# A planner's lists for the first layer, drawn up anew, with some order-only waits taken out

## The chip, the cores and the metric

The kernel runs on one core of a Trainium2 chip. The core has five engines with a queue of instructions each: TensorE (PE in the profile, its weight loads PEld), VectorE (DVE), ScalarE (ACT), GpSimd (POOL) and SyncE (SP), which here only issues DMAs. They are kept in step by semaphores. The metric is the device time of one execution in microseconds (us), from the launch to the last store.

## The reference

The input is x, 2048 rows of 512 values. Two kinds of blocks, A and B, are applied in turn, A B A B, each on a layernorm of its input, and each is added to its input.

```python
def _A_ref(x, wqkv, wo):            # H = 32 heads of Dh = 16
    q, k, v = ...                   # (x @ wqkv), split by head
    phi = lambda t: jnp.where(t > 0, t + 1, jnp.exp(t)) + 1e-6
    pq, pk = phi(q), phi(k)
    kv = jnp.einsum("bhsd,bhse->bhde", pk, v)
    z = jnp.einsum("bhsd->bhd", pk)
    num = jnp.einsum("bhqd,bhde->bhqe", pq, kv)
    den = jnp.einsum("bhqd,bhd->bhq", pq, z)[..., None] + 1e-6
    return (num / den) ... @ wo     # heads joined again

def _B_ref(x, w1, w2):              # 512 -> 1376 -> 512
    return jnp.maximum(x @ w1, 0) @ w2

x = x + _A_ref(_layernorm(x), wqkv, wo)
x = x + _B_ref(_layernorm(x), w1, w2)
x = x + _A_ref(_layernorm(x), wqkv, wo)
x = x + _B_ref(_layernorm(x), w1, w2)
```

A is a linear attention: no softmax over the rows, but a 16x16 matrix kv for each head, summed over all rows, which every row's phi(q) is then multiplied with.

## The kernel before, in words

**Tiles.** The 2048 rows are 16 tiles of 128 rows, and four tiles are a chunk. xin holds x in bf16, xn the normalized tiles, Tb their transposes, which the projections need as an operand. Products go to one of eight PSUM banks (ps), and ScalarE or VectorE brings them from there to SBUF.

**The first layer.** Chunk 0 (tiles 0 to 3) goes a way of its own. Its tiles are only centred (`center`, L855), transposed on TensorE (L524) and brought to Tb (`trev`, L528 and L529), and the reciprocal deviation rstd is put in later, as a scale of the evacuation. For that each tile has an own eps and an own power on GpSimd (`rstd_own`, L849 and L851). Tiles 0 to 2 have their mean and variance from bn_stats and bn_aggr on VectorE (L458, L459), tile 3 from two passes of ScalarE (L865, L867) and two small steps of GpSimd (L869, L871). Chunks 1 to 3 are normalized in full before they are transposed: bn_stats and bn_aggr of each tile on VectorE, eps on GpSimd (`veps`, L464), the power -1/2 on GpSimd (`rstd`, L466), and the normalization on VectorE (`norm`, L490). Chunk 1 does this in two pairs of tiles (4 and 5, 6 and 7) and is transposed on TensorE; chunks 2 and 3 do it four tiles at a time and are transposed by DMA.

The bn_stats of a tile in chunks 1 to 3 reads its tile of xin, and it is also told that it reads the eps result of the tile pair or chunk before (`ln_stats_first(i, [("veps1", lo - 1)])`). It doesn't use that value: this is a wait for the order alone. Tiles 4 and 5 so wait for tile 3's eps, 6 and 7 for that of 4 and 5, chunk 2 for that of 6 and 7, chunk 3 for that of chunk 2.

**phi.** Each block of k or q in a PSUM bank is brought to SBUF as phi by `phi_evac`. The usual way has two passes of ScalarE over the bank, one for t + 1 + 1e-6 (`_lin`, L551) and one for exp (`_exp`, L553), then min(exp, 1) + 1e-6 on VectorE (`_em`, L555), and the larger of both on VectorE (`_phi`, L562). Blocks that are named in the set STT leave the first pass out: VectorE takes t from the bank itself, in one scalar_tensor_tensor (L559). Before, there are two such blocks.

**After the projections** phi(k) and the rows give G (`a_g`), from it kv (`a_kv`), masked on VectorE (L650), and Mf, which is kv times wo (L657, L658). The denominators are products with a column of sums (`den`), ln and exp on ScalarE (L705, L707), spread over partitions by DMAs (`spread`, L717) and multiplied to phi(q) on VectorE (`pqs`, L723). Then come the final products with Mf (`fin`) and the residual (L580). All matmuls but warm ones and transposes are on L569.

**What sets the order.** All operations of all layers are put in a graph with their reads and writes, and with a duration for each that is a constant of the kernel. `_list_schedule` then draws up the list of each engine before anything is emitted: it goes through simulated time and takes for each engine the first operation in order of priority that can start at once, else the one that can start first. The priority is the operation's place in the program plus a number from HINTS (negative is earlier). SEQS fixes the beginning of an engine's list: each name there must come after the one before it. Durations, HINTS and SEQS so change the lists, the banks and the waits that follow from them, and no instruction's own work. Names in HINTS have the layer ahead; all those that differ are of layer 0.

SP issues the loads in the order of the program: x tile 0, x tiles 1 to 3, the key weights in two halves, chunk 1 of x, the query weights, chunks 2 and 3, the value weights, their last row (`ld_wvl`), wo.

Of the kernel before, what the change touches and what calls it, by code (L numbers as in the profile page):

```python
# [7 lines left out]
ALU = alu_op_type.AluOpType  # L8
# [4 lines left out]
PE, ACT, DVE, POOL, SP = "pe", "act", "dve", "pool", "sp"  # L13
# [31 lines left out]
WINDOW = {PE: 64, ACT: 80, DVE: 80, POOL: 12, SP: 6}  # L45


HINTS = {"0.bnag1": -115, "0.bnst15": 29, "0.bnst2": -502, "0.bnst9": -79, "0.den1": 160, "0.den2": -340, "0.g0_2_1": 107,
# [5 lines left out]

SEQS = {
    "dve": ["bnst0", "bnag0"],
    "act": ["mean_3", "trev0a", "sq_3", "trev3", "trev1", "k3_exp", "k3_lin", "k1_exp", "k1_lin", "k0_exp", "q0_3_lin",
            "k2_exp", "q0_2_lin", "k2_lin", "trev6", "q0_1_lin"],
    "pool": ["veps_0", "rstd_0", "veps_2", "nm2_3", "veps_1", "var_3", "rstd_1", "veps_3", "rstd_3", "rstd4", "veps6",
            "rstd_2"],  # L60
    "pe": ["trp0a", "warm2"],
}

STT = {"0.q2_0", "0.q3_2"}


class _Op:
# [22 lines left out]
class _Graph:  # L90
# [14 lines left out]
    def add(self, eng, emit, reads=(), writes=(), dur=100.0, lat=0.0, dma=False, name=""):  # L105
        op = _Op(eng, emit, tuple(reads), tuple(writes), dur, lat, dma, name)
        op.idx = len(self.ops)
        op.key = "%d.%s" % (self.layer, name)
        op.prio = op.idx + HINTS.get(op.key, 0)
        deps = {}  # L110
# [163 lines left out]
def build_kernel(nc, A_x, A_wqkv, A_wo, B_w1, B_w2, out, n_layers_pairs=2, A_PE_CHUNKS=0, windows=None,  # L274
# [14 lines left out]
    EPS = 1e-5  # L289
# [5 lines left out]
    with es:  # L295
        def sb(name, shape, dt):
            return es.enter_context(nc.sbuf_tensor(name, list(shape), dt))
# [33 lines left out]
        var = sb("var", [128, NT], F32)  # L331
        veps = sb("veps", [128, NT], F32)
# [3 lines left out]
        mv = sb("mv", [128, NT, 2], F32)  # L336
# [11 lines left out]
        g = _Graph()  # L348
# [17 lines left out]
        def dma(emit, reads, writes, xfer_ns, name, issue=C_SP_ISSUE, late=0.0):  # L366
            sem = es.enter_context(nc.semaphore("dsem%d" % len(dma_sems)))
            dma_sems.append(sem)

            def _emit(eng, emit=emit, sem=sem):  # L370
                return emit(eng).then_inc(sem, 16)
            op = g.add(SP, _emit, reads, writes, dur=issue, lat=xfer_ns, dma=True, name=name)
            op.seq = sem
            op.late = late
            return op
# [17 lines left out]
        def tok_view(buf, t, lo=0, hi=4):  # L393
            if t == 0 and lo == 0:
                assert hi == 1
                return buf[0][0:128].rearrange("(p n) d -> p n d", p=128)
            if t == 0:
                return buf[0][128:512].rearrange("(p n) d -> p n d", p=128)[:, lo - 1:hi - 1, :]
            return buf[0][512 * t:512 * t + 512].rearrange("(p n) d -> p n d", p=128)[:, lo:hi, :]

        def ld_x(t, lo=0, hi=4, lat=1300.0):
            dma(lambda e: e.dma_start(xin[:, 4 * t + lo:4 * t + hi, :], tok_view(A_x, t, lo, hi)),  # L402
                [], [("xin", i) for i in range(4 * t + lo, 4 * t + hi)], lat, "ld_x%d_%d" % (t, lo))
        ld_x(0, 0, 1, 100.0)
        wq_v = A_wqkv.rearrange("(c p) n -> p c n", p=128)
        ld_x(0, 1, lat=1300.0)
        for k in range(2):
            dma(lambda e, k=k: e.dma_start(wqkv[:, 2 * k:2 * k + 2, D:2 * D], wq_v[:, 2 * k:2 * k + 2, D:2 * D]),
                [], [("wk", k)], 1350.0 - 150.0 * k, "ld_wk%d" % k)
        ld_x(1, lat=1450.0)  # L410
        dma(lambda e: e.dma_start(wqkv[:, :, 0:D], wq_v[:, :, 0:D]), [], [("wq",)], 1550.0, "ld_wq")
        for t in range(2, NCH):
# [44 lines left out]
        def ln_stats_first(i, after=()):  # L457
            g.add(DVE, lambda e: e.bn_stats(bst[:, i, :], xin[:, i, :]), [("xin", i)] + list(after), [("bst", i)], C_DVE_BNST, name="bnst%d" % i)  # L458
            g.add(DVE, lambda e: e.bn_aggr(mv[:, i, :], bst[:, i, :]), [("bst", i)], [("mean", i), ("var", i)], C_DVE_SMALL, name="bnag%d" % i)  # L459

        def ln_part_first(lo, hi):
            sl = slice(lo, hi)
            tl = range(lo, hi)
            g.add(POOL, lambda e: e.tensor_scalar(veps[:, sl], mv[:, sl, 1], 0.0, EPS, ALU.max, ALU.add),  # L464
                  [("var", i) for i in tl], [("veps1", i) for i in tl], 330.0, name="veps%d" % lo)
            g.add(POOL, lambda e: e.tensor_tensor(rstd[:, sl], veps[:, sl], nhalf[:, 0:hi - lo], ALU.pow),  # L466
                  [("veps1", i) for i in tl] + [("nhalf",)], [("rstd", i) for i in tl], 480.0 + 150.0 * (hi - lo), name="rstd%d" % lo)

# [69 lines left out]
        def phi_evac(b, dst_ap, dst_key, name, tok=None):  # L538
# [5 lines left out]
            else:  # L544
                esc, ekey = xres[:, s - NSCR, 0:256].bitcast(BF16), ("xres", s - NSCR)
            stt = "%d.%s" % (g.layer, name) in STT
            sc = 1.0 if tok is None else rstd[:, tok:tok + 1]
# [55 lines left out]
        def ones_col(t):  # L603
            tl = range(4 * t, 4 * t + 4)
            g.add(POOL, lambda e: e.memset(xn[:, 4 * t:4 * t + 4, D - 1:D], 1.0),
                  [], [("xn", i) for i in tl], C_POOL_SMALL, name="onec%d" % t)
# [241 lines left out]
        def rstd_own(i, var_ap):  # L848
            g.add(POOL, lambda e: e.tensor_scalar(veps[:, i:i + 1], var_ap, 0.0, EPS, ALU.max, ALU.add),  # L849
                  [("var", i)], [("veps1", i)], 300.0, name="veps_%d" % i)  # L850
            g.add(POOL, lambda e: e.tensor_tensor(rstd[:, i:i + 1], veps[:, i:i + 1], nhalf[:, 0:1], ALU.pow),  # L851
                  [("veps1", i), ("nhalf",)], [("rstd", i)], C_POOL_POW1, name="rstd_%d" % i)

        def center(i, mu):
            g.add(DVE, lambda e: e.tensor_scalar(xn[:, i, :], xin[:, i, :], mu, None, ALU.subtract),  # L855
                  [("xin", i), ("mean", i)], [("xn", i)], C_DVE_NORM_BF, name="cent%d" % i)
            transpose_pe(i)

        def ln_first(t):
            if t == 0:  # L860
                for i in range(3):
                    ln_stats_first(i, [])
                    rstd_own(i, mv[:, i, 1:2])
                    center(i, mv[:, i, 0:1])
                g.add(ACT, lambda e: e.activation(sqscr[:, 0, :], xin[:, 3, :], ACTF.Identity, scale=INV_D, accum_out=mean[:, 3:4]),  # L865
                      [("xin", 3)], [("sqscr", 0), ("mean", 3)], C_ACT_SB_AP, name="mean_3")
                g.add(ACT, lambda e: e.activation(sqscr[:, 1, :], xin[:, 3, :], ACTF.Square, scale=INV_D ** 0.5, accum_out=s2[:, 3:4]),  # L867
                      [("xin", 3)], [("sqscr", 1), ("s2", 3)], C_ACT_SQ, name="sq_3")
                g.add(POOL, lambda e: e.tensor_tensor(nm2[:, 3:4], mean[:, 3:4], mean[:, 3:4], ALU.mult),  # L869
                      [("mean", 3)], [("nm2", 0)], 300.0, name="nm2_3")  # L870
                g.add(POOL, lambda e: e.tensor_tensor(var[:, 3:4], s2[:, 3:4], nm2[:, 3:4], ALU.subtract),  # L871
                      [("s2", 3), ("nm2", 0)], [("var", 3)], 200.0, name="var_3")
                rstd_own(3, var[:, 3:4])
                center(3, mean[:, 3:4])
                return
            step = 2 if t < FIRST_PE_CHUNKS else 4
            for lo in range(4 * t, 4 * t + 4, step):
                for i in range(lo, lo + step):
                    ln_stats_first(i, [("veps1", lo - 1)])
                ln_part_first(lo, lo + step)  # L880
            for i in range(4 * t, 4 * t + 4):
                ln_norm(i, True)
                if t < FIRST_PE_CHUNKS:
                    transpose_pe(i)
            if t >= FIRST_PE_CHUNKS:
                tr_dma(t, 2 if t == 2 else 1)
            ones_col(t)
# [3 lines left out]
        def tr_dma(t, parts=1):  # L891
            extra = list(ALL_LOADS) if tr_state["first"] else []
            tr_state["first"] = False
            transpose_chunk(t, extra, parts)
            tr_state["last"] = g.ops[-1]
# [16 lines left out]
        for t in range(3):  # L912
            ln_first(t)
# [255 lines left out]
```

## Time and profile before

| What | us |
|---|---|
| Median of three runs | 589.03 |
| Lowest and highest of them | 281.23, 1539.66 |
| Profiled execution, device time | 280.72 |
| Its span, first to last instruction | 279.0 |
| TensorE busy | 273.4 |
| ScalarE busy | 173.2 |
| VectorE busy | 141.1 |
| GpSimd busy | 50.5 |

The granted clock of TensorE was 1.00 throughout. The span is the time from the first to the last instruction; 1.7 us of the device time lie around it. Busy times are sums over the span, and engines overlap. A matmul's row is longer than its turn (0.379 us for 512 columns, though the next one starts 0.216 us later), since it counts the way through the array; so TensorE's waits are read from the starts of its matmuls.

What lands when, from the DMAs' issues and landings in the trace: tile 0 at 2.81 us, tiles 1 to 3 at 4.63, the key weights' halves at 5.32 and 6.55, chunk 1 at 7.84, the query weights at 9.29, chunk 2 at 10.57, chunk 3 at 11.92.

The first layer's A block fills about the first 57 us of TensorE's list, mixed with the beginning of what follows.

### The profile page before, as it was taken

The page shows a single profiled execution, that of the slowest core. Times are in us where ns is not written, and L with a number is a line of the kernel's source. Part 1 is how long each engine was busy: PE and PEld are TensorE (multiplying, and loading weights), DVE is VectorE, ACT ScalarE, POOL GpSimd, SP SyncE. Part 2 cuts the span into 40 slices and gives each one's busy share as a digit, 9 for nine tenths or more (in the row PEclk, how much of TensorE's full clock was granted, in tenths as well). Part 3 has the DMA queues.
Part 4 walks back from the last instruction along what each step waited for, and adds up shares of the span by engine and source line. Part 5 has one row for each costly group of instructions (what it writes and reads, how often), then busy time and mean ns, then how long its engine had stood idle before and what let it go on. Part 6 is the DMA issues. An engine that isn't in the chain of part 4 may idle for free.

```text
span 279.0 us, 4188 instructions
## 1 busy us (share of the span) xinstructions
PE 273.4 (98%) x1553; PEld 140.4 (50%) x1573; DVE 141.1 (51%) x378; ACT 173.2 (62%) x353; POOL 50.5 (18%) x132
## 2 busy tenths in 40 slices
PE   7999999999999999999999999999999999999996
PEld 3545557546544544544454455664554554454443
DVE  5899983899401362443363477279935300120222
ACT  4999996669773682677372799765884366226000
POOL 6532000035400160400040400003236100000000
DMA  7905496655810053070003030085431642021012
GB/s 225 378 19 79 89 295 197 156 124 79 152 36 0 2 94 75 1 96 0 0 8 69 0 75 0 2 187 116 78 76 22 164 80 21 0 75 22 0 75 75
DMA packets 46356, 22.62 MB, mean 81 GB/s; under 512 B 36640, under 2 KB 44800, under 8 KB 46336
## 3 DMA queue, kind: packets, MB, share of 16 engines
q1 hardware_dynamic: 46336, 22.35, 34.7%
q8 instruction: 12, 0.20, 0.3%
q14 instruction: 8, 0.07, 0.1%
HBM read 7.14 MB, written 2.10 MB: 33 GB/s over the span
## 4 chain that ended last, share of the span: by engine, by line
PE 92%; DVE 3%; DMA 1%; POOL 1%; ACT 1%; issue 1%; SPq 0%
PE ps L569 92%; DVE bst L458 2%; DMA xin<-in_A_x_dram 1%; ACT big L551 1%; POOL veps L464 0%; ACT escr L553 0%; DVE Tb L529 0%; POOL rstd L851 0%; PE ps L524 0%; DVE mv L459 0%; SPq L402 0%; DVE xn L490 0%; DVE xin L818 0%; POOL veps L849 0%; POOL var L871 0%
## 5 line engine op out<-in xcount | busy, mean ns | idle before, releaser
L569 PE MATMUL ps<-w,big 128*128 128x512 bf16 (+3 forms) x356 | 76.3, 372 | 0.4
L569 PE MATMUL ps<-Tb,w 128*128 128x512 bf16 (+1 forms) x352 | 70.8, 360 | 0.0
L798 ACT ACTIVATE big<-ps 128x512 bf16<-128x512 f32 x71 | 42.2, 596 | 24.3 <-PE ps L569 24.2
L569 PEld LDWEIGHTS ps<-w,big 128*128 128x128 bf16 (+1 forms) x363 | 35.0, 98 | 41.2 <-ACT big L798 0.3
L569 PEld LDWEIGHTS ps<-Tb,w 128*128 128x128 bf16 x352 | 34.0, 98 | 32.8
L586 ACT ACTIVATE sqscr<-xres 128x512 bf16<-128x512 f32 x48 | 29.9, 623 | 30.1 <-DVE xres L580 29.7
L580 DVE SCALAR_TENSOR_TENSOR xres<-ps,xres 128x512 f32<-128x512 f32 x32 | 21.2, 689 | 43.2 <-PE ps L569 43.2
L551 ACT ACTIVATE big<-ps 128x512 bf16<-128x512 f32 x54 | 34.3, 634 | 3.0 <-PE ps L569 3.0
L577 DVE TENSOR_TENSOR xin<-ps,xres 128x512 bf16<-128x512 f32 x15 | 10.4, 691 | 49.7 <-PE ps L569 49.7
L569 PE MATMUL ps<-wqkv,Tb 128*128 128x512 bf16 x139 | 32.8, 379 | 0.5 <-ACT Tb L528 0.3
L569 PE MATMUL ps<-big,xn 128*128 128x256 bf16 (+1 forms) x222 | 30.4, 287 | 0.1
L553 ACT ACTIVATE escr<-ps 128x512 bf16<-128x512 f32 x44 | 27.9, 635 | 1.2 <-PE ps L569 1.2
L569 PE MATMUL ps<-Tb,wqkv 128*128 128x512 bf16 x112 | 26.6, 379 | 0.0
L569 PEld LDWEIGHTS ps<-big,xn 128*128 128x128 bf16 x224 | 21.6, 98 | 9.0 <-issue 0.8
L472 POOL TENSOR_SCALAR mean<-s 128x4 f32<-128x4 f32 x12 | 3.0, 248 | 121.1 <-DVE xres L580 121.0
L569 PE MATMUL ps<-Mf,big 128*128 128x512 bf16 x109 | 24.7, 379 | 0.2
L555 DVE TENSOR_SCALAR escr<-escr 128x512 bf16<-128x512 bf16 x52 | 14.9, 290 | 18.7 <-ACT escr L553 18.3
L562 DVE TENSOR_TENSOR big<-big,escr 128x512 bf16<-128x512 bf16 x51 | 21.2, 421 | 1.1
L569 PEld LDWEIGHTS ps<-wqkv,Tb 128*128 128x128 bf16 x144 | 13.8, 98 | 15.8 <-ACT Tb L528 0.6
L499 ACT ACTIVATE xn<-xres,nbias,rstd 128x512 bf16<-128x512 f32 x15 | 11.9, 815 | 8.8 <-POOL nbias L484 8.8
L569 PEld LDWEIGHTS ps<-Mf,big 128*128 128x128 bf16 x112 | 10.8, 98 | 13.0 <-ACT Mf L657 0.2
L494 DVE TENSOR_SCALAR xn<-xres,mean,rstd 128x512 bf16<-128x512 f32 x23 | 15.1, 687 | 3.7 <-POOL nbias L484 3.6
(92 smaller groups left out, 226.9 us busy)
## 6 DMA issues: line engine op xcount, KB each, us to landing
big<-rdc SPq DMA_DIRECT2D x32, 128.0 KB, 2.7
xin<-in_A_x_dram SPq DMA_DIRECT2D x3, 512.0 KB, 6.9
w<-in_B_w_dram SPq DMA_DIRECT2D x1, 1376.0 KB, 7.1
w<-in_B_w_dram SPq DMA_DIRECT2D x1, 1280.0 KB, 10.6
wqkv<-in_A_wqkv_dram SPq DMA_DIRECT2D x2, 512.0 KB, 7.3
out_dram<-xin SPq DMA_DIRECT2D x2, 512.0 KB, 2.8
wqkv<-in_A_wqkv_dram SPq DMA_DIRECT2D x2, 256.0 KB, 4.0
wo<-in_A_wo_dram SPq DMA_DIRECT2D x1, 512.0 KB, 8.6
```

The costliest lines, as they stand in the source:

```text
L458: g.add(DVE, lambda e: e.bn_stats(bst[:, i, :], xin[:, i, :]), [("xin", i)] + list(after), [("bst", i)], C_DVE_BNST, name="bnst%d" % i)
L494: ts = (POOL, lambda e: e.tensor_scalar(xn[:, i, :], src, mean[:, i:i + 1], rstd[:, i:i + 1], ALU.add, ALU.mult), C_POOL_NORM)
L499: (ACT, lambda e: e.activation(xn[:, i, :], src, ACTF.Identity, scale=rstd[:, i:i + 1], bias=nbias[:, i:i + 1]), C_ACT_SB_AP)],
L551: g.add(ACT, lambda e: e.activation(dst_ap, psv[:, b, :], ACTF.Identity, bias=1.0 + 1e-6, scale=sc), [("ps", b)] + rk, [dst_key], C_ACT_PS ...
L553: g.add(ACT, lambda e: e.activation(esc, psv[:, b, :], ACTF.Exp, scale=sc), [("ps", b)] + rk, [ekey], C_ACT_EXP + xd, name=name + "_exp")
L555: g.add(DVE, lambda e: e.tensor_scalar(esc, esc, 1.0, 1e-6, ALU.min, ALU.add), [ekey], [ekey], C_DVE_BF4X, name=name + "_em")
L562: g.add(DVE, lambda e: e.tensor_tensor(dst_ap, dst_ap, esc, ALU.max), [dst_key, ekey], [dst_key], 340.0, name=name + "_phi")
L569: last = e.matmul(o, l, r, start=st, stop=sp, skip_group_check=skip)
L577: g.add(DVE, lambda e: e.tensor_tensor(xin[:, i, :], psv[:, b, :], src, ALU.add), [("ps", b), skey], [("xin", i)], C_DVE_PSUM, name="resid ...
L580: g.add(DVE, lambda e: e.scalar_tensor_tensor(xres[:, i, :], psv[:, b, :], 0.0, src, ALU.add, ALU.add, accum_out=s1[:, i:i + 1]), [("ps", ...
L586: g.add(ACT, lambda e: e.activation(sqscr[:, q, :], xres[:, i, :], ACTF.Square, accum_out=s2[:, i:i + 1]), [("xres", i)], [("sqscr", q), ( ...
L798: g.add_flex([(ACT, lambda e, M=M, b=b, u=u: e.activation(unit_ap(u, M), psv[0:M, b, :], ACTF.Relu), C_ACT_PSUM), (DVE, lambda e, M=M, b=b ...
```

## The change

Five edits, all in the first layer:

- The bn_stats of chunks 1 to 3 are no longer told to read the eps result before them.
- The eps of chunk 1 (tiles 4 and 5, tiles 6 and 7) is done by VectorE instead of GpSimd. Those of chunks 2 and 3 stay on GpSimd, and their duration for the planner goes from 330 to 400 ns.
- Six blocks instead of two take the way with scalar_tensor_tensor: k15, q2_2, q2_3 and q3_0 are added.
- HINTS of layer 0 are replaced, and SEQS are changed: GpSimd's list is fixed for two names only, TensorE's second name is the second pair of transposes instead of the small warm matmul, and ScalarE's order differs from its sixth name on.
- The planner's transfer times of x tiles 1 to 3 and of the key weights are others. The DMAs themselves are the same.

```diff
-HINTS = {"0.bnag1": -115, "0.bnst15": 29, "0.bnst2": -502, "0.bnst9": -79, "0.den1": 160, "0.den2": -340, "0.g0_2_1": 107,
...
+HINTS = {"0.bnag10": -258, "0.bnag12": 39, "0.bnst10": 11, "0.cent2": -484, "0.den1": 266, "0.fin1_2": -193, "0.fin2_0":
+         -113, "0.fin2_2": 4, "0.fin3_0": -728, "0.g0_2_3": 102, "0.g1_0_0": 63, "0.g1_2_0": 120, "0.k12_lin": 13,
...
+         -8, "0.ld_wvl": 152, "0.mev0": 161, "0.norm1": -42, "0.pqs2_2": 127, "0.pqs2_3": -755, "0.q0_0_exp": 281,
...
+         "0.spread0_0": -232, "0.spread0_1": -146, "0.spread0_2": -63, "0.spread0_3": -978, "0.spread1_3": -63,
+         "0.spread2_0": -512, "0.spread2_3": -59, "0.tr0_0": -824, "0.trq": -6, "0.veps4": -713, "0.veps_2": 301, "0.warm2":
...
 SEQS = {
     "dve": ["bnst0", "bnag0"],
-    "act": ["mean_3", "trev0a", "sq_3", "trev3", "trev1", "k3_exp", "k3_lin", "k1_exp", "k1_lin", "k0_exp", "q0_3_lin",
-            "k2_exp", "q0_2_lin", "k2_lin", "trev6", "q0_1_lin"],
-    "pool": ["veps_0", "rstd_0", "veps_2", "nm2_3", "veps_1", "var_3", "rstd_1", "veps_3", "rstd_3", "rstd4", "veps6",
-            "rstd_2"],
-    "pe": ["trp0a", "warm2"],
+    "act": ["mean_3", "trev0a", "sq_3", "trev3", "trev1", "k3_lin", "k3_exp", "k1_exp", "k0_exp", "k2_lin", "k1_lin",
+            "q0_2_lin", "trev6", "q0_3_lin", "k5_lin", "k4_exp", "k2_exp", "q0_1_exp"],
+    "pool": ["veps_0", "rstd_0"],
+    "pe": ["trp0a", "trp0b"],
 }
 
-STT = {"0.q2_0", "0.q3_2"}
+STT = {"0.k15", "0.q2_0", "0.q2_2", "0.q2_3", "0.q3_0", "0.q3_2"}
...
-        ld_x(0, 1, lat=1300.0)
+        ld_x(0, 1, lat=1550.0)
...
-                [], [("wk", k)], 1350.0 - 150.0 * k, "ld_wk%d" % k)
+                [], [("wk", k)], 1050.0 + 150.0 * k, "ld_wk%d" % k)
...
         def ln_part_first(lo, hi):
...
-            g.add(POOL, lambda e: e.tensor_scalar(veps[:, sl], mv[:, sl, 1], 0.0, EPS, ALU.max, ALU.add),
-                  [("var", i) for i in tl], [("veps1", i) for i in tl], 330.0, name="veps%d" % lo)
+            eng, cost = (DVE, 95.0) if lo < 8 else (POOL, 400.0)
+            g.add(eng, lambda e: e.tensor_scalar(veps[:, sl], mv[:, sl, 1], 0.0, EPS, ALU.max, ALU.add),
+                  [("var", i) for i in tl], [("veps1", i) for i in tl], cost, name="veps%d" % lo)
...
-                    ln_stats_first(i, [("veps1", lo - 1)])
+                    ln_stats_first(i)
```

10 rows, old and new, of the table HINTS are left out of this document.

## The prediction

> **What bounds the kernel now.** I read the page's head first, for the share of each engine.
>
> ```profile
> span 279.0 us, 4188 instructions
> PE 273.4 (98%) x1553; PEld 140.4 (50%) x1573; DVE 141.1 (51%) x378; ACT 173.2 (62%) x353; POOL 50.5 (18%) x132
> ```
>
> TensorE is busy for 98% of the span: only 279.0 − 273.4 = 5.6 us are idle, and a matmul's modelled end hides short waits. So I then read the chain that ended last.
>
> ```profile
> 1.25 3.38 DMA xin<-in_A_x_dram
> ...
> 10.21 0.67 POOL veps L464
> 10.90 1.29 DVE bst L458 x2
> ...
> 12.75 0.72 POOL veps L464
> 13.49 0.69 DVE bst L458
> ...
> 14.51 0.60 DVE bst L458
> 15.11 0.33 DVE xn L490
> 15.48 0.40 PE ps L524 x4
> ...
> 54.89 0.25 issue
> ```
>
> Up to 15.48 us the chain runs over VectorE and GpSimd, through the very waits that the change drops (eps at 10.21, then the next two bn_stats; eps at 12.75, then the next). From 15.48 on it is TensorE to the end, but for six evacuations at 127.9 to 130.4, during which TensorE has no gap.
>
> Third, TensorE's own timeline, for the waits behind modelled ends.
>
> ```profile
> 5.32 0.27 PE L524 MATMUL ps<-ident,xn 128*128 128x128 bf16 x2
> 5.84 0.60 PE L569 MATMUL ps<-wqkv,Tb 128*128 128x512 bf16 x2 [0.26 <-ACT Tb L528]
> 6.31 0.92 PE L524 MATMUL ps<-ident,xn 128*128 128x128 bf16 x8
> ...
> 13.36 1.89 PE L569 MATMUL ps<-wqkv,Tb 128*128 128x512 bf16 x8
> 15.48 0.40 PE L524 MATMUL ps<-ident,xn 128*128 128x128 bf16 x4 [0.23 <-DVE xn L490]
> ...
> 55.14 1.67 PE L569 MATMUL ps<-Mf,xres 128*128 128x512 bf16 x7 [0.25 <-DVE Mf L658]
> ```
>
> Matmuls of 512 columns start 0.216 us apart where nothing waits (16 of them at 18.53 fill 3.62 us: 15 x 0.216 and one whole one of 0.38), transposes 0.056 us apart. Any longer step is a wait; where the step is exactly one matmul more, a record is missing. Four waits are left in the whole span: **W1** 0.42 us before 5.84 (the first evacuation on ScalarE), **W2** 0.29 us at 6.55 to 6.84 (a centred tile from VectorE), **W3** 0.39 us before 15.48 (normalized tile 6), **W4** 0.32 us before 55.14 (Mf). Together 1.42 us. Beside them stand only the 5.05 us before the first transpose and the 2.4 us after the last matmul, and the change touches neither: the nine warm matmuls run from 1.24 to 5.05 in both. So the change can gain about 1.4 us at most, 0.5% of the span. A gain over 2% (5.6 us), which is about what a measurement of this kernel can tell from no change, isn't to be had from the schedule.
>
> The other two engines tell where it could lose.
>
> ```profile
> 8.00:16.00 8.00, 7.71 (x45) 3.71 (x45) 7.72 (x25) 7.59 (x14) 3.84 (x7) 1.00 0.84 302
> 16.00:24.00 8.00, 7.95 (x46) 4.23 (x46) 8.00 (x27) 8.00 (x17) 1.54 (x4) 1.00 0.39 55
> ...
> 28.00:36.00 8.00, 7.95 (x41) 4.02 (x41) 8.00 (x30) 7.47 (x16) 0.12 (x1) 1.00 0.57 108
> 36.00:40.00 4.00, 4.00 (x26) 2.41 (x25) 3.36 (x10) 3.81 (x9) 0.00 (x0) 1.00 0.99 270
> ```
>
> These are stretches: after the length come the columns PE, weight loads, VectorE, ScalarE, GpSimd, granted clock, DMA. From 8 to 36 us VectorE and ScalarE are as full as TensorE. Yet ScalarE waits for TensorE at 25.65 (0.16 us) and 34.30 (0.53), so TensorE leads.
>
> **The parts, against this execution's own 280.72 us** (the span and 1.7 us around it). The runs without a profile gave 281.23, 589 and 1540; nothing in the profile makes the two long ones, so I forecast an execution like the profiled one.
>
> *Dropped waits and eps on VectorE (W3).* Today tile 7's bn_aggr ends at 12.66; eps on GpSimd runs 12.75 to 13.46; then GpSimd takes tile 2's power first (13.43, 0.54) and tiles 6 and 7's at 13.94 (0.70), so rstd is there at 14.64. VectorE meanwhile does two bn_stats of chunk 2 (13.49 and 14.43, 0.69 and 0.68) and normalizes tile 6 at 15.03. After the change eps is a 128x2 instruction on VectorE, which the trace doesn't show there. Its nearest rows are the accumulator read of 128x1 (0.08) and bn_aggr, which writes 128x2 (median 0.17); I take 0.12, nearer to bn_aggr's output size than to its six inputs. Two of them cost 0.24 us of VectorE (0.16 to 0.34). Then: 12.66 + 0.12, a hop of 0.09 (as 12.66 to 12.75), the power 0.70, a hop of 0.03 (as 7.81 to 7.84): rstd at 13.6. With one bn_stats (0.68) in the way, the normalization (0.38 and 0.07 to TensorE) ends at 14.7, before TensorE runs dry at 15.09. W3 goes: −0.39. That TensorE starts only 0.4 us earlier and not 1 is because its matmuls end at 15.09; they are the cover. Bounds: −0.39, and +1.36 if two more bn_stats get ahead (below).
>
> A word on the prices: GpSimd's eps of two columns took 0.66 and 0.71 us, those of four 0.32 and 0.47. The Trainium skill's SBUF — State Buffer, "Who interferes with whom", says that GpSimd is fully blocked while VectorE runs a two-port instruction or one with two SBUF inputs. The trace agrees: at 10.34 and 12.58 to 13.36 VectorE ran just such. By that rule the power can be blocked in eps's stead, by up to the 0.48 us of a pair of such instructions; rstd at 14.1 still leaves W3 gone, unless a bn_stats also starts in between.
>
> *Lists of the first microseconds (W1, W2).* W1 stays: the first evacuation still follows the mean on ScalarE in its list, and 512 columns of mean end at 5.38. The small warm matmul goes out from between the two pairs of transposes, 0.11 us that lies in W1 anyway. W2 can shrink, since the second bn_stats is no longer drawn ahead of the centring; but half of the keys' weights lands at 6.55 and holds what could fill it. −0.1 (0 to −0.29).
>
> *Six STT.* Each of the four new ones takes a 512-column pass from ScalarE (pitch 0.48 us) and turns VectorE's maximum (pitch 0.33) into one from PSUM (0.69 long, pitch 0.61 at 49.91): ScalarE −1.9 us, VectorE +1.1. Two (q2_2, q2_3) fall into the full stretch up to 36 us, 0.56 us; VectorE's idle 0.64 us from 36 to 40 takes them up. Those of q3_0 and k15 fall near 38 to 42, with 2.1 us idle from 40 to 44. I count 0. Without that cover: +0.56. ScalarE's relief buys nothing, as it already waits for TensorE; should it free a bank earlier, −0.2.
>
> *Orders of 40 to 57 us (W4).* Mf's, the final products' and the spreads' places change. W4 is a chain kv, mask, product, copy, and can fall or return: 0 (−0.32 to +0.32). A lone den costs 0.09 before and 0.11 after it on TensorE's steps (51.36 to 51.90), and now two lie together at 44.49; den1 is put off, so it may stand alone: +0.1 (0 to +0.2). On SP the queue is empty from 39.3 to 46.4 and each spread takes some 0.65 us; a spread drawn ahead of one that is needed costs one such step, hidden here by VectorE's backlog of products at 50.5 to 54.8. The last-column load wvl, put behind, landed at 13.76 and is first read at 33.09: 0. The changed times of x and key loads are the planner's alone: 0.
>
> Sum: −0.39 − 0.1 + 0 + 0 + 0.1 = −0.4, **280.3 us**.
>
> **Rivals.** *All waits but W1 go*: −0.39 −0.29 −0.32 = −1.0, 279.7; with W1, 279.3. For it: the chain goes through the dropped waits. Against: W1 and W4 aren't made by them.
>
> *The dropped wait was a guard* (the slower side). Chunk 2 lands at 10.57, so all four of its bn_stats can run before tile 6's normalization, where today two do. Place: VectorE, 12.1 to 15.0 us. Each more costs 0.68, so W3 grows by up to 2 x 0.68 = 1.36; with the 0.24 of eps and the 0.56 of STTs uncovered, 280.72 + 2.2 = 282.9. It decides when a third bn_stats of chunk 2 starts before tile 6's normalization. For it: VectorE is 96% full there, and the wait ahead of 15.48 shows that its order counts. Against: GpSimd's shorter way leaves less time for them.
>
> *The clock opens late.* TensorE's warm matmuls start 0.427 us apart up to 5.05, then 0.216. Should the faster pace come one such stretch (3.8 us) later, the work of 5.05 to 8.9 less W1 and W2 doubles: +3.1, 283.8. The Trainium skill's TensorE: Matmul & The Clock Gate, Part 1, says that the gate opens after some 3.4 us of sustained work in a free-running window; by its figure the nine matmuls' 3.8 us just suffice, and the trace agrees.
>
> *The change does next to nothing*: lists differ, TensorE is fed alike, 280.7.
>
> **Chances.** Forecast (279.9 to 280.6) 0.40; most waits go (279.3 to 279.9) 0.13; next to nothing (280.6 to 281.2) 0.20; guard and VectorE late (281.2 to 282.9) 0.15; clock 0.02; an order that starves TensorE by over 5.6 us 0.04. The rest, 0.06, is a comparison caught by something like the two long runs; since those are of before, I give 0.04 of it to faster and 0.02 to slower. The range takes in the first four, 279.2 to 282.7. Faster by over 2%: 0.04; slower by over 2%: 0.04 + 0.02 = 0.06 (the clock's 283.8 is within 2%); within: 0.90.
>
> **What would show it.** After the change: bn_stats of tiles 6 and 7 straight behind those of 4 and 5 with no eps between; eps among VectorE's rows at 0.08 to 0.17 us and only two groups of four on GpSimd; the transposes now at 15.48 without a wait; first wait still 0.4 us before 5.8; six STT rows; TensorE's steps 0.216 us elsewhere; span 278.3 to 278.9. I am wrong if TensorE waits anew between 16 and 57 us, above all for VectorE, or if tile 6's normalization is later than 15.1.

## The result, and the profile after

The change makes the kernel slower, by half a per cent: 282.39 us, median of ten runs (281.79 to 284.14), against 281.25 before. The ratio, that of the means, is 1.0054 with a 95% interval of 1.0031 to 1.0077; the two long runs of before, 589 and 1540 us, are left out of it, and nothing like them came again. The forecast was 280.3 in a range of 279.2 to 282.7. The time lies in the range, the sign was wrong.

The profiled execution after took 281.79 us, 1.07 more than the one before. The head of its page:

```profile
span 280.1 us, 4212 instructions
PE 274.7 (98%) x1573; PEld 139.9 (50%) x1573; DVE 140.2 (50%) x378; ACT 172.3 (62%) x351; POOL 52.7 (19%) x130
```

ScalarE and VectorE have each lost 0.9 us of work. GpSimd has two instructions fewer and yet is busy 2.2 us longer (50.5 before). That is the first sign of where the time went. The second is TensorE's own timeline:

```profile
5.62 0.60 PE L575 MATMUL ps<-wqkv,Tb 128*128 128x512 bf16 x2 [0.25 <-ACT Tb L534]
6.08 0.92 PE L530 MATMUL ps<-ident,xn 128*128 128x128 bf16 x12
...
14.13 0.39 PE L530 MATMUL ps<-ident,xn 128*128 128x128 bf16 x4
...
21.08 2.35 PE L575 MATMUL ps<-big,xn 128*128 128x512 bf16 x16 [0.29 <-DVE big L568]
...
34.42 3.63 PE L575 MATMUL ps<-wqkv,Tb 128*128 128x512 bf16 x16 [1.05 <-DMA Tb<-xn]
...
56.02 1.90 PE L575 MATMUL ps<-Mf,xres 128*128 128x512 bf16 x8
```

The transposes before 7 us now stand in one row of twelve, tile 6's at 14.13 don't wait, nor does the product with Mf at 56.02. But two waits are there that before hasn't: ahead of 21.08 for a maximum of VectorE, and ahead of 34.42 for a DMA. By the starts of the matmuls they are 0.46 and 1.21 us. The whole account, from those starts:

| TensorE | before | after |
|---|---|---|
| First transpose | 5.05 | 4.87 |
| W1 | 0.42 | 0.42 |
| W2, and two small steps beside it | 0.29 | 0.06 |
| Transposes of tiles 4 and 5 | 0.00 | 0.33 |
| W3, transposes of tile 6 | 0.40 | 0.00 |
| Ahead of 21.08 | 0.00 | 0.46 |
| Ahead of 34.42 | 0.00 | 1.21 |
| W4 (see below) | 0.10 | 0.00 |

The waits grow by 1.27, the first transpose is 0.18 earlier, so 1.09 is left, and the last matmul does start 1.10 us later (277.43 against 276.33). All of it arises before 58 us. The earlier start is not the change's: TensorE's faster pace came within the ninth of the warm matmuls instead of after it. Part of W2's gain may be chance as well: in before_copy3, the unchanged kernel once more (below), only 0.10 us was lost at its place.

The chain that ended last says what stands behind the longer wait. Columns: start, length, what.

```profile
25.05 2.48 POOL veps L470
27.53 0.07 POOL xn L611
27.60 0.02 issue
27.61 1.04 POOL rstd L472
28.66 0.03 issue
28.68 1.38 DVE xn L496 x4
30.06 0.03 DVE xres L561
30.09 4.28 DMA Tb<-xn
34.37 0.05 issue
34.42 243.25 PE ps L575 x1403
```

Read it backwards: TensorE goes on at 34.42 because chunk 3's transposes land at 34.37; they were issued at 30.09, behind its normalization; that waited for the power; the power waited for chunk 3's eps, **a GpSimd instruction on 128x4 numbers, which took 2.48 us**. In before the same instruction took 0.47, the transposes were issued at 28.44 and landed at 32.67. From before's timeline, VectorE and GpSimd:

```profile
24.98 0.39 DVE L562 TENSOR_TENSOR big<-big,escr 128x512 bf16<-128x512 bf16 x1
25.14 0.47 POOL L464 TENSOR_SCALAR veps<-mv 128x4 f32<-128x4 f32 x1 [6.03 <-DVE mv L459]
25.29 0.49 DVE L555 TENSOR_SCALAR escr<-escr 128x512 bf16<-128x512 bf16 x2
...
25.70 1.30 POOL L466 TENSOR_TENSOR rstd<-veps,nhalf 128x4 f32<-128x4 f32 x1
```

The same stretch after, with what ran beside eps:

```profile
24.88 0.46 DVE L561 TENSOR_SCALAR escr<-escr 128x512 bf16<-128x512 bf16 x2
25.05 2.48 POOL L470 TENSOR_SCALAR veps<-mv 128x4 f32<-128x4 f32 x1 [5.71 <-DVE mv L464]
25.25 1.09 DVE L568 TENSOR_TENSOR big<-big,escr 128x512 bf16<-128x512 bf16 x3
26.26 0.49 DVE L561 TENSOR_SCALAR escr<-escr 128x512 bf16<-128x512 bf16 x2
26.67 0.75 DVE L568 TENSOR_TENSOR big<-big,escr 128x512 bf16<-128x512 bf16 x2
...
27.61 1.03 POOL L472 TENSOR_TENSOR rstd<-veps,nhalf 128x4 f32<-128x4 f32 x1
28.68 1.38 DVE L496 TENSOR_SCALAR xn<-xin,mv,rstd 128x512 bf16<-128x512 bf16 x4 [1.26 <-POOL rstd L472]
```

VectorE works without a gap from 24.88 to 27.42 (26.67 + 0.75), on fast copies (its step min(exp, 1) + 1e-6, L561) and on maxima (L568), and eps ends at 27.53, 0.11 later. Then the power takes its usual 1.03, and VectorE, which has nothing else left, waits 1.26 us for it. Chunk 2 shows the same with the power, 2.50 us instead of before's 1.04 (at 18.07):

```profile
16.56 0.41 DVE L906 TENSOR_SCALAR xn<-xin,mv,rstd 128x512 bf16<-128x512 bf16 x1
16.77 2.50 POOL L472 TENSOR_TENSOR rstd<-veps,nhalf 128x4 f32<-128x4 f32 x1
16.88 0.30 DVE L561 TENSOR_SCALAR escr<-escr 128x512 bf16<-128x512 bf16 x1
17.08 1.10 DVE L568 TENSOR_TENSOR big<-big,escr 128x512 bf16<-128x512 bf16 x3
18.09 0.30 DVE L561 TENSOR_SCALAR escr<-escr 128x512 bf16<-128x512 bf16 x1
```

It starts beside a normalization; VectorE's row of fast copies and maxima lasts to 18.39, and the power ends at 19.27, 0.88 us behind it: nearly all of the usual 1.0 us is done behind the row. VectorE then waits 0.93 for it, normalizes chunk 2, and only behind that takes the maximum of key block 2 (20.60), for which TensorE's products at 21.08 wait.

### The profile page after: what moved, and what is told of

Read it like the earlier page. It is cut to its first block, busy times and chain, and to the rows that moved or that the text cites. A ratio compares the mean times of both kernels' runs of the same rounds, so it can differ in the third digit from the quotient of the medians.

```text
span 280.1 us, 4212 instructions
## 1 busy us (share of the span) xinstructions
PE 274.7 (98%) x1573; PEld 139.9 (50%) x1573; DVE 140.2 (50%) x378; ACT 172.3 (62%) x351; POOL 52.7 (19%) x130
## 4 chain that ended last, share of the span: by engine, by line
PE 87%; DMA 4%; DVE 3%; POOL 2%; issue 2%; SPq 1%; POOLq 0%
PE ps L575 87%; DMA xin<-in_A_x_dram 2%; DVE bst L463 2%; DMA Tb<-xn 2%; POOL rstd L472 1%; POOL veps L470 1%; DVE xn L496 1%; SPq L413 0%; SPq L407 0%; DVE mv L464 0%; DVE escr L561 0%; DVE Tb L535 0%; DVE xn L906 0%; DVE xin L824 0%; POOL xn L611 0%
## 5 line engine op out<-in xcount | busy, mean ns | idle before, releaser
L575 PE MATMUL ps<-w,big 128*128 128x512 bf16 (+3 forms) x363 | 77.4, 373 | 0.0
L804 ACT ACTIVATE big<-ps 128x512 bf16<-128x512 f32 x71 | 42.2, 596 | 23.9 <-PE ps L575 23.8
L557 ACT ACTIVATE big<-ps 128x512 bf16<-128x512 f32 x50 | 30.8, 627 | 2.6 <-PE ps L575 2.6
L561 DVE TENSOR_SCALAR escr<-escr 128x512 bf16<-128x512 bf16 x52 | 14.8, 291 | 18.3 <-ACT escr L559 18.1
L568 DVE TENSOR_TENSOR big<-big,escr 128x512 bf16<-128x512 bf16 x49 | 20.2, 423 | 1.1
```

The costliest lines, as they stand in the source:

```text
L557: g.add(ACT, lambda e: e.activation(dst_ap, psv[:, b, :], ACTF.Identity, bias=1.0 + 1e-6, scale=sc), [("ps", b)] + rk, [dst_key], C_ACT_PS ...
L561: g.add(DVE, lambda e: e.tensor_scalar(esc, esc, 1.0, 1e-6, ALU.min, ALU.add), [ekey], [ekey], C_DVE_BF4X, name=name + "_em")
L568: g.add(DVE, lambda e: e.tensor_tensor(dst_ap, dst_ap, esc, ALU.max), [dst_key, ekey], [dst_key], 340.0, name=name + "_phi")
L575: last = e.matmul(o, l, r, start=st, stop=sp, skip_group_check=skip)
L804: g.add_flex([(ACT, lambda e, M=M, b=b, u=u: e.activation(unit_ap(u, M), psv[0:M, b, :], ACTF.Relu), C_ACT_PSUM), (DVE, lambda e, M=M, b=b ...
```

## The experiments

The theory to be tested: GpSimd's small instructions stand still while VectorE runs its copies (min(exp, 1) + 1e-6) and its maxima of two SBUF operands back to back; the two new waits, 1.67 us, come from that alone. The rivals are that the new order of the lists makes them by itself, that the STTs do, and, later, that the loads do. Kernels of one group ran on the same chip, and each group has its own runs of before (medians 281.33, 281.37, 282.09; in the last group single executions). After's own ten runs belong to none of these groups, so ratios to before compare better with its 1.0054 than medians do. "Finished lists" means that the planner's lists were kept and only the named step was moved in them.

### First group

**one_input.** The lists of after, untouched; eight maxima of the first layer are replaced by an instruction of like length with one operand, so that this part of phi is left out.

```diff
-                g.add(DVE, lambda e: e.tensor_tensor(dst_ap, dst_ap, esc, ALU.max),
+                # k3, k0, k1, k4, q0_1, k6, k7, k5 of layer 0
+                g.add(DVE, lambda e: e.bn_stats(alone[:, n, :], esc[:, 0:256]),
```

> The changed kernel, with its lists untouched. Only eight of VectorE's maxima of the first layer (of k3, k0, k1 at 17.1 us and of k4, q0_1, k6, k7, k5 at 25.2 to 27.4) are each replaced by a bn_stats over 256 columns of the same exponential, which takes about the same turn of VectorE (0.33 us) but reads one SBUF operand. So these eight blocks keep t + 1 + 1e-6 and are not compared with the exponential: this part of phi is left out. Theory (GpSimd is held off while VectorE runs instructions with two SBUF operands or fast copies back to back): chunk 2's power falls from 2.50 to at most 1.6 us, chunk 3's eps from 2.48 to at most 0.8, and TensorE's waits of 0.46 us at 20.6 and 1.21 at 33.2 fall below 0.2 together; time 1.2 to 1.7 us below the changed kernel, 280.7 to 281.2. Rival (VectorE has too much to do, or its order is late; GpSimd is long for another reason): VectorE's load and order are the same, so the power and eps stay at 2.5 and the time at 282.4.

Measured: 280.75 (280.51 to 281.35), ratio 0.9983 [0.9969, 0.9997], 1.64 us below after's median (of another group). GpSimd and VectorE in its timeline:

```profile
24.13 0.46 DVE L563 TENSOR_SCALAR escr<-escr 128x512 bf16<-128x512 bf16 x2
24.30 0.40 POOL L472 TENSOR_SCALAR veps<-mv 128x4 f32<-128x4 f32 x1 [5.88 <-DVE mv L466]
24.50 1.07 DVE L572 BATCH_NORM_STATS2 alone<-escr 128x6 f32<-128x256 bf16 x3
...
24.78 1.23 POOL L474 TENSOR_TENSOR rstd<-veps,nhalf 128x4 f32<-128x4 f32 x1
```

Same order, same lengths on VectorE (1.07 against 1.09), but one SBUF operand: eps takes 0.40 instead of 2.48, and chunk 2's power 1.29 instead of 2.50. Both new waits are gone. So it is not the lists' order by itself.

**eps_pause.** In after's finished lists, the eps of chunks 2 and 3 go to VectorE, each followed by an added bn_stats of 192 columns, a pause in which GpSimd can begin its power.

```diff
+move("0.veps8", DVE, "0.bnag10");  move("0.veps12", DVE, "0.bnag12")   # finished lists; condensed
+# and behind each:  e.bn_stats(alone[...], xin[:, 0, 0:192])
```

> The changed kernel with its lists untouched but for two places: eps of chunk 2 and of chunk 3 move from GpSimd to VectorE, right behind the last bn_aggr of their chunk, and behind each stands an added bn_stats of 192 columns that nobody reads (0.26 us), so that the power on GpSimd can start beside an instruction with one SBUF operand. Everything is computed. Theory (held off at the start): the power of chunk 2 takes 1.0 to 1.7 us, that of chunk 3 1.0 to 2.0, it ends 0.7 to 1.2 us earlier than in the changed kernel, and the two new waits of TensorE fall from 1.67 us to 0.3 to 0.8; time 281.2 to 281.6. Rival (VectorE's load): two eps and two pauses add 0.8 us to VectorE, so the time stays at 282.4 or grows to 283.

Measured: 280.96 (280.57 to 281.42), ratio 0.9984 [0.9959, 1.0009]. The powers took 1.06 us (chunk 2) and 1.01 (chunk 3); of the two waits 0.28 us at 28.2 is left. The time is a little below the expected 281.2 to 281.6, though this execution also waited 0.77 us for key weights at 7.2.

**after_stt2.** After with two STTs instead of six, its lists drawn anew.

```diff
-STT = {"0.k15", "0.q2_0", "0.q2_2", "0.q2_3", "0.q3_0", "0.q3_2"}
+STT = {"0.q2_0", "0.q3_2"}
```

> The changed kernel with the two blocks of before on the way with scalar_tensor_tensor instead of six; the planner draws its lists anew from that, which differ mostly behind 29 us. Theory (GpSimd held off at 16.8 and 25.1 us): both waits stay, as they are made before the first of the four; time 282.2 to 282.7. Rival (the six passes overload VectorE, the forecast's uncovered 0.56 us): 0.5 us or more below, 281.9 or less.

Measured: 283.55 (282.35 to 284.26), ratio 1.0075 [1.0048, 1.0102]. The power took 2.50 and eps 2.48 as in after, with waits of 0.68 and 1.40; so the STTs don't make them. A third wait, 1.27 us, came up, which no theory had. VectorE's timeline:

```profile
41.72 1.43 DVE L606 TENSOR_TENSOR wqkv<-wqkv,wvl 128x512 bf16<-128x512 bf16 x4 [1.93 <-DMA wvl<-in_A_wqkv_dram]
43.07 0.42 DVE L568 TENSOR_TENSOR big<-big,escr 128x512 bf16<-128x512 bf16 x1
```

VectorE's list comes to the instruction that uses wvl before wvl is there: its load stands behind the transposes of q on SP, issued at 35.71. VectorE waits 1.93 us, and the maxima behind it come late for TensorE's products at 44.20. After has the same late load (issued 35.62, landed 41.58), and VectorE waits 0.97 us for it there too, but TensorE has other work.

**before_late_eps.** The reverse: before's finished lists, in which chunk 3's eps also waits for key block 4's maximum, and so starts inside VectorE's row.

```diff
+after_op("0.veps12").sdeps.append(after_op("0.k4_phi"))                # finished lists
```

> The kernel before, lists untouched; only chunk 3's eps on GpSimd also waits for the maximum of k4 on VectorE (order only, 0.25 us later), so that it starts into VectorE's unbroken run of fast copies and maxima at 25.4 to 26.9 instead of ahead of it. Theory (held off): eps grows from 0.47 to 1.3 to 2.0 us, the power ends at 28.0 to 28.4 instead of 27.0, the normalization of chunk 3 starts 1.0 to 1.4 us later; its transposes land at 33.7 to 34.1 against TensorE's need at 34.1, so the time moves by 0 to 0.3 us only. Rival (GpSimd's long steps have to do with the new lists, not with VectorE's instructions): eps stays at 0.5 and all comes 0.25 us later; no change of time.

Measured: 281.8 (281.6 to 282.9), ratio 1.0020 [1.0006, 1.0034]. Started at 25.49 instead of 25.14, eps took 1.50 instead of 0.47, again until 0.11 us behind the row's end. Thus 0.35 us later was enough to triple it. The price was under-estimated, since it fell in another place: products behind the late normalization waited 0.96 us at 28.7, not those behind the transposes.

### Second group

**eps_dve.** As eps_pause, without the pauses.

> The changed kernel with eps of chunks 2 and 3 on VectorE right behind their last bn_aggr, lists otherwise untouched: the run with the pauses without its pauses. Theory (GpSimd needs a moment in which VectorE leaves the second SBUF port, to begin): chunk 2's power starts beside a copy out of PSUM and takes 1.0 to 1.4 us; chunk 3's starts into fast copies and maxima and takes 2.2 us or more, ending near 28.3, so of the two waits the first (0.46 us) goes and 0.8 to 1.2 of the second stays; time 281.6 to 282.1. Rival (moving eps was all, the added pauses did nothing): both powers 1.0 to 1.3 us, time 280.8 to 281.1 as with the pauses.

Measured: 281.02 (280.55 to 281.85), ratio 0.9991 [0.9975, 1.0008]; powers 1.01 and 1.01, both waits gone. The pause was not needed, and with it falls my refinement that a power begun in the row would be caught: chunk 3's began at 25.56, among copies (25.39 to 25.90), with three maxima behind them. (The profiled execution, 281.65, lost 0.94 us ahead of 8.29 to late key weights.)

**eps_pause2.** As eps_pause, with pauses of 96 columns and the maximum of q0_1 behind chunk 3's normalization.

> The run with the two pauses, made leaner: the added bn_stats take 96 columns instead of 192, and the maximum of q0_1 on VectorE, which only a much later transpose needs, moves from ahead of k6's maximum to behind the normalizations of chunk 3, so that k5's maximum is ready earlier for TensorE's sums. Everything is computed. Theory: powers stay at 1.0 to 1.2 us, TensorE's wait of 0.28 us at 28.1 goes; time 280.5 to 280.9, that is 0.997 to 0.999 of before. Rival (a pause of 0.1 us less is too short for GpSimd to begin): chunk 3's power at 2 us or more and the time at 281.5 or more.

Measured: 280.76 (280.26 to 281.77), ratio 0.9988 [0.9974, 1.0001]; powers 1.01 and 1.14. As expected, and no better than eps_dve by more than the intervals.

**before_nowaits** and **before_epsdve** do one part of the change alone, in before, with the lists drawn anew.

```diff
-                    ln_stats_first(i, [("veps1", lo - 1)])      # before_nowaits
+                    ln_stats_first(i)
...
+            eng, cost = (DVE, 95.0) if lo < 8 else (POOL, 330.0)  # before_epsdve; veps6 out of SEQS
+            g.add(eng, lambda e: e.tensor_scalar(veps[:, sl], ...), cost, name="veps%d" % lo)
```

> The kernel before with the order-only waits dropped and nothing else; the planner draws its lists anew. Theory (the wait of chunk 3's first bn_stats for chunk 2's eps had put an instruction with one SBUF operand beside chunk 2's power): without it the planner puts chunk 2's eps and power beside normalization, fast copies and maxima; the power grows from 1.04 to 1.8 to 2.5 us, and the time by 0.3 to 0.8 us, to 281.6 to 282.1. Rival (the forecast: these waits only cost): chunk 1's normalization comes earlier, W3 goes, the power stays at 1.0 to 1.3, time 280.9.

> The kernel before with chunk 1's two eps on VectorE (and that name taken out of GpSimd's fixed list) and nothing else; the planner draws its lists anew. All theories: eps takes 0.15 us of VectorE as in the changed kernel, tile 6 is normalized 0.5 to 1 us earlier and W3 (0.39 us) goes. Theory of the held-off GpSimd: chunk 2's eps and power stay by chunk 3's first bn_stats as before, at 0.3 and 1.0 us, so the time is 280.8 to 281.1. Rival (moving eps is what made the loss): 281.6 or more.

Measured: before_nowaits 282.9 (282.03 to 283.37), ratio 1.0048 [1.0028, 1.0069]; before_epsdve 282.4 (281.91 to 283.21), ratio 1.0038 [1.0023, 1.0053]. Each part alone takes W3 away and each alone makes the kernel slower. In the first, eps of chunks 2 and 3 took 1.53 and 1.81 (I had expected the power to be caught, and 281.6 to 282.1); TensorE lost 0.46 us ahead of 22.74 and 1.08 ahead of 31.18, and in this execution 1.09 more ahead of 7.76, for late key weights, which isn't the edit's. In the second, where I had expected a gain, 1.08 and 2.01, and TensorE lost 1.70 us at 28.3, from its timeline and GpSimd's:

```profile
25.34 2.01 POOL L465 TENSOR_SCALAR veps<-mv 128x4 f32<-128x4 f32 x1 [5.52 <-DVE mv L459]
...
30.26 1.04 PE L570 MATMUL ps<-big,xn 128*128 128x512 bf16 x4 [1.54 <-DVE big L563]
```

I had thought of chunk 1 alone once more. With the lists redrawn, chunk 3's eps began 0.2 us later than in before, beside a copy and a maximum, and was held.

### Third group

**before_alleps.** before_epsdve, and in its finished lists the eps of chunks 2 and 3 go to VectorE as well.

```diff
+for name, behind in (("0.veps8", "0.bnag11"), ("0.veps12", "0.bnag15")):
+    move(name, DVE, behind)                                            # finished lists
```

> The kernel before with chunk 1's two eps on VectorE, as in the run of that part alone, and then in its finished lists also those of chunks 2 and 3 moved from GpSimd to VectorE, right behind the last bn_aggr of their chunk; nothing else differs. Theory (an eps on GpSimd gets caught in VectorE's unbroken run): chunk 3's power ends near 26.5 us instead of 28.45, TensorE's wait of 1.70 us at 28.6 falls to 0.3 or less; time 280.6 to 281.0, 1.4 to 1.8 below the part alone. Rival (the lists that the planner drew are late for another reason): 282 or more.

Measured: 280.85 (280.45 to 281.14), ratio 0.9957 [0.9943, 0.9971]. VectorE and GpSimd in its timeline:

```profile
24.75 0.17 DVE L465 TENSOR_SCALAR veps<-mv 128x4 f32<-128x4 f32 x1
24.82 0.29 DVE L556 TENSOR_SCALAR escr<-escr 128x512 bf16<-128x512 bf16 x1
25.00 1.01 POOL L467 TENSOR_TENSOR rstd<-veps,nhalf 128x4 f32<-128x4 f32 x1 [0.23 <-DVE veps L465]
```

0.17 us of VectorE in place of 2.01 of GpSimd, and the 1.70 us wait is down to 0.09. It is faster than before on the same chip, and its median lies 1.54 below after's, though those two weren't run side by side.

**before_eps23.** The same move in before's own lists, nothing else.

> The kernel before, lists untouched but for eps of chunks 2 and 3, which move from GpSimd to VectorE right behind the last bn_aggr of their chunk. Theory: in the kernel before these two got through in 0.32 and 0.47 us by their place, so nothing is to be gained there: powers 1.0 to 1.3 us, W1 to W4 as before, time within 0.3 us of before, 281.0 to 281.6. Rival (GpSimd's eps always costs): 0.5 us or more below before.

Measured: 280.92 (280.70 to 281.84), ratio 0.9966 [0.9950, 0.9982]. The time is that expected; the ratio isn't, because before itself had 282.09 on this chip. The theory gives no gain here, as before's eps isn't held.

**after_stt2_eps.** after_stt2 with the move of eps8 and eps12.

> The run with two scalar_tensor_tensor blocks instead of six, with eps of chunks 2 and 3 moved to VectorE in its finished lists. Theory: its first two waits (0.68 and 1.40 us) go; the third (1.27 us, at 42.9), where VectorE stands in front of the last products waiting for the late load of the value weights' last row, becomes shorter by the time that the load's forerunners on SP, the chunk 3 and query transposes, come earlier, but doesn't go; time 281.0 to 281.8. Rival (four more passes of ScalarE are what costs 1 us): the time stays 1 us above the like run with six, at 282 or more.

Measured: 281.79 (281.11 to 282.41), ratio 0.9994 [0.9979, 1.0009], 1.76 below after_stt2. The first two waits are gone, the third (0.83) stays.

**eps_dve2.** eps_dve, with q0_1's maximum as in eps_pause2 and the load of wvl back behind that of the value weights.

> The changed kernel with eps of chunks 2 and 3 on VectorE without pauses, the maximum of q0_1 moved behind the normalizations of chunk 3, and the load of the value weights' last row put back behind the value weights on SP. Everything is computed. Theory: both new waits stay away, k5's maximum is 0.33 us earlier, and VectorE's wait of 0.9 us for that load goes, which nobody behind it was waiting for; time 280.5 to 280.9. Rival (without a pause chunk 3's power is caught in some executions): the median at 281 or more, with a wider spread.

Measured: 281.02 (280.12 to 281.79), ratio 0.9963 [0.9946, 0.9981]. Powers of 1.01, no wait of the two; a little above what I expected, with 0.5 us for key weights in its list of waits, and a step 0.70 us too long on TensorE at 59.5. The median meets the rival's 281 too; that no power was caught is known of the profiled execution alone.

### Fourth group: before itself

**before_copy1, before_copy2, before_copy3** are before, unchanged, one execution each: was its GpSimd caught at times, which would explain the gain of before_eps23?

> The kernel before, unchanged, looked at again: in one profile chunk 3's eps took 0.47 us, yet its executions lie between 280.4 and 283 us, and moving only eps of chunks 2 and 3 brought 0.3% on a chip on which before took 282.1. Theory (whether GpSimd's eps begins is a matter of some 0.1 us, so before is caught in a part of its executions): in a profile with a device time of 281.7 or more, eps of chunk 2 or 3 takes 1.0 us or more; in one of 281.2 or less it takes 0.5 or less. Rival (the chip or the loads differ): eps stays at 0.3 to 0.5 us in the long ones too, and their time is lost in waits for loads.

> As the run before it: a second look at the unchanged kernel before. Long (281.7 us or more) with eps of 1.0 us or more, or short (281.2 or less) with eps of 0.5 or less, by the theory; by its rival eps has nothing to do with it.

> As the two runs before it: a third look at the unchanged kernel before, with the same expectations.

Measured: 281.76, 282.41 and 281.09. In all three, as in the first profile, eps took 0.32 and 0.47 and the powers 1.04 and 1.30. So that was wrong. What differs lies in the first microseconds, and it is of two kinds. One is when the first loads land: the keys' second half at 6.50, 8.37 and 6.82, chunk 1 of x at 9.24, 9.67 and 8.43. In before_copy2 TensorE waits 1.58 us by its starts for the keys, and this is the largest of its waits (in total, times, longest):

```profile
PE ps L569 <- DMA wqkv<-in_A_wqkv_dram: 1.9, 2, 1.4
```

The other is when TensorE takes up its faster pace. In before_copy1 the slow one lasts to 7.30 us: transposes start 0.107 us apart and the first two products take 1.03 us, not 0.60 as in before_copy3, where the faster pace came at 5.01. Their lines, copy1 first:

```profile
5.95 1.03 PE L569 MATMUL ps<-wqkv,Tb 128*128 128x512 bf16 x2
...
5.76 0.60 PE L569 MATMUL ps<-wqkv,Tb 128*128 128x512 bf16 x2 [0.26 <-ACT Tb L528]
```

Of the 0.70 us by which TensorE's last matmul is later in before_copy1 than in before_copy3, 0.60 have arisen by the products behind those transposes (6.87 in before_copy3). The profile's granted clock reads 1.00 all the while; the pace is seen in the starts alone.

The loads and the pace account for most of the spread between these executions. Whether they also make the 0.3% of before_eps23 isn't shown. In none of the four profiles of before does TensorE wait for chunk 3's transposes (in before_copy2 they land at 33.88, and the next product with Tb starts at 34.44 without a wait), so an earlier power should have gained nothing there.

## Why the prediction was wrong, point by point

**What bounds the kernel** held. TensorE was the bound, and no version tried gains more than the 1.42 us of waits that were listed. (Two small things in it were wrong: the measurement tells far less than 2% from no change, as the ratio's interval reaches 0.23% to each side, and the evacuations in the chain at 127.9 to 130.4 are five, not six.) One of the waits was misread. W4 was given as 0.32 us ahead of 55.14; TensorE's weight loads in before show that a matmul record was lost just there:

```profile
54.91 1.41 PEld L569 LDWEIGHTS ps<-Mf,xres 128*128 128x128 bf16 x8 [0.32 <-DVE Mf L658]
```

Eight loads, but the row at 55.14 has seven matmuls. One of 0.216 us stood in the gap, and W4 was 0.10 (0.10 too in before_copy1 and before_copy3, with all eight recorded). The rule in the prediction caught lost records only where a step was exactly one matmul too long, not where one hid in a wait.

**Dropped waits and eps on VectorE** is the step that failed. What it priced came out: eps took 0.15 us on VectorE (0.12 taken), the normalization of tile 6 started at 13.55 instead of 15.03, and W3 went. TensorE could not use all of it, as it now reached tiles 4 and 5 earlier and waited 0.33 there, which the step didn't count; chunk 1 of x also landed 0.60 us later in this execution (8.44 against 7.84), so not all of that wait need be the change's. But the failure is in what was left out: chunks 2 and 3 keep their eps and powers on GpSimd, and their cost was taken as unchanged because their code is. Their neighbours on VectorE changed. The prediction even quoted the rule at stake, the Trainium skill's SBUF — State Buffer, "Who interferes with whom", by which GpSimd stands still while VectorE has the ports that they share. The trace agrees (eps ends 0.11 us behind the row's end), but I applied it to chunk 1's power only and bounded it by one pair of instructions, 0.48 us. Measured: 2.0 us for chunk 3's eps and 1.5 for chunk 2's power, because the row had no gap, and 1.67 us of TensorE for both. With that term the forecast's sum of −0.4 would have been +1.3; the profiled executions differ by +1.07. The prediction's own sign of being wrong, that TensorE waits anew between 16 and 57 us, did come.

**The guard rival** had the sign, but neither its place nor its mechanism. Two bn_stats of chunk 2 stand ahead of tile 6's normalization (at 11.61 and 12.98), as many as in before, and no third. before_nowaits shows that the dropped waits did keep something: when they alone are taken out, eps of chunks 2 and 3 fall into VectorE's row. before_epsdve, which keeps these waits and loses about as much, shows that another redrawing of the lists can do it too. The planner gives eps a constant 330 or 400 ns, so it can't see it.

**Lists of the first microseconds**: W1 stayed, W2 shrank by 0.23 instead of 0.1 (part of it perhaps chance, as said above). **Orders of 40 to 57 us**: the lone den of +0.1 didn't come (the same three groups in both), and W4 went.

**Six STT** was mis-sized, and the late load of **wvl** with it. Counted at 0 and 0. In these lists six look better than two, by 0.6 (ratios 1.0054 and 1.0075, with intervals that overlap) to 1.2 us (medians of different groups); where the two waits are taken away, 281.02 against 281.79 of eps_dve2 and after_stt2_eps on one chip, though these differ by two more moves. What two STTs meet is the wait for wvl, which the prediction dismissed by its landing in before, at 13.76, without looking where the load would go on SP: it moved 28 us.

**The clock rival** didn't occur in the profile after, where the faster pace came at 4.87. But the nine warm matmuls' 3.8 us don't always suffice: in before_copy1 the pace came 2.2 us later than in before, and against before_copy3 this cost 0.6 us by the starts, not 3.1. That **the change does next to nothing** is out, as 1 lies outside the interval.

## What to carry to other kernels

A tiny instruction on GpSimd has no price of its own: beside an unbroken row of VectorE copies and two-operand maxima, an eps of 0.25 to 0.47 us took up to 2.48 us, and all that waits for it moves. When lists are redrawn, look at every instruction of that engine whose neighbours change, not only at the edited ones; where one feeds the path, put it on VectorE (0.17 us here). Before a wait is read from the starts of matmuls, count the weight loads beside it. And before two executions are compared, see when their first loads landed and when TensorE took up its pace: together they can move a time by more than this change.

## What was not expected of the hardware

An eps that is caught is held to the end of the row, not to the end of the instruction it meets:

| kernel, chunk | eps starts | took | VectorE's row ends | eps ends behind it |
|---|---|---|---|---|
| after, 3 | 25.05 | 2.48 | 27.42 | 0.11 |
| before_epsdve, 3 | 25.34 | 2.01 | 27.24 | 0.11 |
| before_nowaits, 3 | 26.45 | 1.81 | 28.15 | 0.11 |
| before_late_eps, 3 | 25.49 | 1.50 | 26.88 | 0.11 |
| before_epsdve, 2 | 17.62 | 1.08 | 18.57 | 0.13 |

Not always, though. before's own eps of chunk 3 began at 25.14 beside a maximum (24.98 to 25.37), in a row that lasted to 26.85, and was done in 0.47; that of chunk 2 in before_nowaits was let in after 1.53 us, with a maximum running (18.83 to 19.24). Powers begun shortly ahead of maxima, at 25.68 in eps_pause and 25.56 in eps_dve, kept their 1.01 through them, while after's at 16.77, begun beside a normalization with copies and maxima behind it, was held. What decides whether one gets in, and whether copies alone would hold it, these runs don't settle.

The other surprise is the first microseconds: in four profiles of the same kernel the keys' second half landed between 6.50 and 8.37 us, and TensorE waited up to 1.58 us for it, which is more than the whole effect that was studied. TensorE's faster pace came as early as 4.5 us in one of them and as late as 7.3 in another, after the same nine warm matmuls.
